# A step list written anew in its first quarter, two fp32 stands a batch instead of three, and scores copied out of PSUM

## The chip, the cores and the metric

The kernel runs on one core of one Trainium2 chip. The metric is the device time of one execution in microseconds (us); three runs of the kernel before gave 703.85, 704.16 and 704.18 us, median 704.16.

## The reference, cut to what matters

```python
# attention over memory slots; B=8 batches, 8 heads, S=576 rows, head dim 64, 32 slots
a = softmax(phi, axis=2)                         # over the rows
k_m, v_m = a^T @ k, a^T @ v                      # 32 slots a head
attn = softmax(q @ k_m^T / 8, axis=-1)           # 576 x 32 a head
x = attn @ v_m                                   # joined to (4608, 512)
h = x @ w_in                                     # (4608, 2048)
g = 0.5 * h * (1 + erf(h / sqrt(2)))
out = g @ w_out                                  # (4608, 512), all in float32
```

## The kernel before, in words

The attention and the first matmul of the feed-forward part are folded together: instead of x the kernel forms U = v_m @ w_in for each batch (32 slots a head, 2048 columns), and h is the product of U and the attention weights p. Both large matmuls keep float32 accuracy by splitting each operand into a high part in FP32R (a float32 format that TensorE takes in one pass) and a low part with the rest, and adding three products: high by high, low by high, high by low.

For a batch b the steps are: load phi, exponentials over the rows (amax, aexp), `slots` (the slot sums k_m and v_m), `km` (scaled copy to SBUF), `slotsT` and `kT` (transposed slots), then for each half of the 576 rows `score` (fp32 matmuls into PSUM), `sT` (transpose by DVE), max, sub, exp, sum, inv, mul, `pT`, and `ph`/`pl` (high and low part of p). `Up.b.f.n` forms n chunks (of 128 columns) of U from chunk f on in fp32, `Uh` and `Ul` split them. For each of 16 chunks f of a batch `h.b.f.hf` is a hidden piece (six FP32R matmuls of 288 columns for one half of the rows), `gelu` writes it to SBUF, `gh`/`gl` split it, and `p.b.f` is a projection (twelve FP32R matmuls of 512 columns into four PSUM banks, acc). `o` copies the sums out. `tp` is the projection of the last 64 rows of two batches. The weights arrive as 64-bit patterns and are decoded once, in the first part, which I call the head: `Lwi.f`/`Lwo.f` load 128 rows, `dB` (two ACT instructions), `dC` (two on DVE), `dS` (DVE), `dDi`/`dDo` (GpSimd, POOL), and for w_out `dE` and `dF`.

The order of all work is written out by hand in ORDER (lines 22 to 202), a list of such steps; the part behind the colon names an engine (a ACT, d DVE) or a kind of PSUM bank (x, y). Lines 1053 to 1057 tie every instruction to the one before it on its engine, the SP queue's DMA issues included, so each engine follows the list strictly, and an instruction that waits holds everything behind it on its engine.

PSUM has eight banks: four for acc (`ps_acc`), two single ones (`ps_h`, kind y), and two that form one tile of a pair (`ps_at`, kind x, line 317). `banks` (line 311) hands them out. A "stand" in this text is a run of fp32 pieces on PE between the FP32R matmuls. From batch 3 on a batch has three: `slots` of the next batch, `score` of half 0 and `Up.b.0.4` (before projection 3 of the batch ahead); `slotsT`, `score` of half 1 and `Up.b.4.4` (before projection 7); `Up.b.8.4` and `Up.b.12.4` (before projection 13). The scores of a half stand in columns 0 to 287 of the two banks, the slot sums of the next batch in columns 384 to 511; `sT` (line 775) and `km` (line 605) read them in PSUM.

SBUF tiles are shared by tag. Tag U (five buffers, NU) holds U tiles, raw weights and later one kv tile a batch; tag kv (eight buffers, NK = NC + 3) holds the ten loads Lkv.1.g.c of batch 1, which slots.1.0 (c of g=0) and slots.1.1 (c of g=1) read (line 569). Warm-up matmuls `W.n` (line 1014) stand in the head where PE would be idle.

Of the kernel before, what the change touches and what calls it, by code (L numbers as in the profile page):

```python
# [23 lines left out]
amax.0.0 aexp.0.0 dC.1.1 Lq.0.0 at.0.0.4 atc.0.0.4:d at.0.0.0 dS.1.1 at.0.1.0 dB.0.1
dC.0.1 dS.0.1 dDo.0 anorm.0 atc.0.1.0:d atc.0.0.0:a Lwi.1 Lwi.0 atc.0.1.4:a dE.0:d
dB.1.0 Lq.0.1 dB.0.0 Lphi.1.0 slots.0.0.0 dF.0 km.0.0.0 slots.0.1.0 Lkv0.1.1 km.0.1.0
Lkv0.0.1 slotsT.0.0 kT.0.0:d dC.1.0 dC.0.0 n_score.0 dS.0.0 dDi.0 n_score.1 n_score.2
n_max.0 n_sub.0 n_exp.0 slots.0.1.1 Lwo.2 Lwi.2 Lkv.1.0.1 amax.1.0 W.1 aexp.1.0 W.3
# [12 lines left out]
max.1.0 Lwi.6 Up.0.4.1 h.0.3.0 dE.4:a Lwo.6 gelu.0.2.1 dC.5.0 gelu.0.2.0 dB.5.1 gh.0.2:a
sub.1.0 exp.1.0 dB.6.1 dF.4 Lwi.7 gl.0.2 dS.5.0 dDi.5 Uh.0.4:d sum.1.0 p.0.1 gelu.0.3.0
Ul.0.4 gelu.0.3.1 Lwo.7 dB.6.0 dC.6.1 Up.0.5.1 dC.5.1 inv.1.0 p.0.2 dS.5.1 Lq.1.1
h.0.4.1 mul.1.0 Uh.0.5:d pT.1.0 dDo.5 Ul.0.5 h.0.4.0 gelu.0.4.1 score.1.1 h.0.5.0
h.0.5.1 dE.5:a dC.6.0 dS.6.0 sT.1.1.1 sT.1.1.0 gh.0.3:a gelu.0.4.0 dDi.6 Up.0.6.1 Lwo.8
gl.0.3 p.0.3 ph.1.0:a dS.6.1 Uh.0.6:a dF.5 Ul.0.6 max.1.1 gh.0.4:a dDo.6 gl.0.4
gelu.0.5.1 Up.1.0.4 Lwo.9 dB.7.0 dE.6:a dC.7.0 h.0.6.1 pl.1.0 gelu.0.5.0 dS.7.0 gh.0.5:a
p.0.4 dDi.7 Uh.1.0 sub.1.1 exp.1.1 Up.0.7.1 Ul.1.0 dB.7.1 gelu.0.6.1 Uh.0.7:a dF.6
h.0.6.0 gl.0.5 p.0.5 sum.1.1 inv.1.1 dC.7.1 dS.7.1 mul.1.1 dB.9.1 Ul.0.7 gelu.0.6.0
dDo.7 h.0.7.0 gelu.0.7.0 pT.1.1 gh.0.6:d h.0.7.1 Up.1.4.4 dC.9.1 gl.0.6 gelu.0.7.1  # L50
ph.1.1:a h.1.0.0 dB.9.0 Lwi.8 dE.7:d gh.0.7:a pl.1.1 gelu.1.0.0 dS.9.1 dB.8.1 p.0.6 dF.7
dB.8.0 h.1.0.1 Uh.1.4:d gl.0.7 gelu.1.0.1 h.1.1.0 dC.9.0 dDo.9 Lwo.10 gh.1.0:a h.1.2.0
dS.9.0 h.1.1.1 dC.8.0 gelu.1.1.0 p.0.7 dC.8.1 dE.9:a dS.8.0 gelu.1.1.1 h.1.2.1 dDi.9
o.0.0.7:a h.1.3.1 gl.1.0 dS.8.1 dF.9 p.1.0 Lwo.11 o.0.1.7:a Ul.1.4 h.1.3.0 gelu.1.2.0
Lwi.10 dDo.8 o.0.2.7:a dB.10.1 h.1.4.1 Lwi.11 gh.1.1:a gelu.1.2.1 o.0.3.7:d dE.8:a
gl.1.1 dDi.8 gelu.1.3.1 dB.10.0 dC.10.1 dS.10.1 dDo.10 gelu.1.3.0 h.1.4.0 gh.1.2:a dF.8
Lwi.14 dB.11.0 gl.1.2 dC.10.0 Lwo.13 p.1.1 Lwi.13 dE.10:d gelu.1.4.0 h.1.5.0 p.1.2
gelu.1.4.1 h.1.5.1 h.1.7.1 dB.11.1 dC.11.0 dF.10 dC.11.1 gh.1.3:a dS.11.1 Lwo.14 gl.1.3
dS.10.0 gelu.1.5.0 dDo.11 dDi.10 p.1.3 h.1.7.0 dB.13.1 dS.11.0 gelu.1.5.1 gh.1.4:d
dDi.11 Up.0.8.4 gl.1.4 gelu.1.7.1 dC.13.1 dE.11:d p.1.4 dF.11 Uh.0.8:a Lwo.12 Lwo.15  # L60
gelu.1.7.0 dB.13.0 h.1.6.1 h.1.6.0 gh.1.5:d dS.13.1 dB.14.1 dDo.13 gl.1.5 Ul.0.8 dC.14.1
h.0.8.0 dS.14.1 h.0.8.1 p.1.5 gelu.1.6.1 dC.13.0 gelu.1.6.0 gh.1.6:a gl.1.6 Up.1.8.4
dB.14.0 gelu.0.8.0 gelu.0.8.1 dS.13.0 h.0.10.1 dDo.14 p.1.6 dC.14.0 dDi.13 Lwi.12
dE.13:d gh.1.7:a h.0.9.0 dE.14:a dF.13 gl.1.7 dS.14.0 Uh.1.8:d dF.14 dB.12.0 dDi.14
p.1.7 dB.12.1 gelu.0.9.0 dC.12.0 dC.12.1 dB.15.1 Lwi.15 gh.0.8:d gl.0.8 dB.15.0 dS.12.0
gelu.0.10.1 Ul.1.8 h.0.10.0 gelu.0.10.0 h.0.9.1 dS.12.1 o.1.2.7:d dDi.12 o.1.1.7:d
dDo.12 gelu.0.9.1 dC.15.0 gh.0.9:a h.0.11.1 Up.0.12.2 o.1.0.7:a h.0.11.0 dS.15.0
o.1.3.7:d gl.0.9 dE.12:d Uh.0.12:d p.0.8 gelu.0.11.0 p.0.9 dC.15.1 gelu.0.11.1 gh.0.10:d
Ul.0.12 dS.15.1 gl.0.10 dDi.15 Lphi.2.1 h.0.13.1 gh.0.11:a dB.15 gl.0.11 Lphin.2
Up.0.14.2 dC.15 h.0.13.0 gelu.0.13.0 Lphi.2.0 Uh.0.14:d amax.2.1 p.0.10 amax.2.0 dF.12  # L70
# [6 lines left out]
gl.1.8 o.0.1.15 Lphi.3.1 Up.1.12.4 gelu.1.10.0 h.1.11.1 Uh.1.12:a p.1.8 gelu.1.10.1
Ul.1.12 slots.2 h.1.11.0 gelu.1.11.1 gelu.1.11.0 km.2.0 km.2.1 gh.1.10:d slotsT.2
amax.3.1 Lphin.3 kT.2:d p.1.9 gl.1.10 score.2.0 Lq.2.1 sT.2.0.1 amax.3.0 h.1.12.1
sT.2.0.0 h.1.12.0 gelu.1.12.0 gelu.1.12.1 Up.2.0.4 p.1.10 max.2.0 Lkv.3.0.3 h.1.13.1  # L80
sub.2.0 aexp.3.1 gh.1.11:d gl.1.11 h.1.13.0 exp.2.0 sum.2.0 inv.2.0 gelu.1.13.0
gelu.1.13.1 Uh.2.0:d gh.1.12:a p.1.11 Ul.2.0 mul.2.0 score.2.1 Lkv.3.0.1 h.1.15.0
# [1041 lines left out]
```

## Time and profile before

| | |
|---|---|
| median of three runs | 704.16 us |
| profiled execution | 704.29 us, span 702.5 us |
| PE busy with matmuls | 687.9 us, 98% of the span |
| DVE, ACT, POOL busy | 400.8, 306.3, 57.0 us |
| granted TensorE clock, mean | 0.997 of full speed |
| moved by DMA | 63.58 MB |

The profile is of one execution. Matmuls are pipelined and their recorded ends are modelled, so a busy PE is one whose matmuls follow each other. L12 is line 12 of the kernel. In a row of the timeline the bracket gives the idle time of the engine ahead of it and what ended it.

### The profile page before, as it was taken

The numbers are of one execution on the slowest core, as the hardware profiler recorded it, in microseconds if no ns is written. First come the engines' busy times: TensorE is split into PE (matmuls) and PEld (weight loads), VectorE is DVE, ScalarE is ACT, GpSimd is POOL, SyncE is SP. The second block draws the span as 40 slices with busy tenths as digits, with TensorE's granted clock in tenths as the row PEclk, the third lists the DMA queues.
The fourth block names the chain that finished last, engine by engine and source line by source line (L and its number), as shares of the span: only waits on it lengthen the run. The fifth ranks groups of instructions, "written<-read, shape, count | busy, mean of one in ns | idle before, by whom it ended". The sixth has DMA issues, their size and how long they took to land.

```text
span 702.5 us, 12355 instructions
## 1 busy us (share of the span) xinstructions
PE 687.9 (98%) x4970; PEld 574.4 (82%) x4970; DVE 400.8 (57%) x757; ACT 306.3 (44%) x692; POOL 57.0 (8%) x42
## 2 busy tenths in 40 slices
...
GB/s 341 341 279 113 121 151 192 61 47 201 132 139 79 188 155 82 61 51 131 57 1 75 67 118 54 1 61 35 35 0 61 16 35 1 1 61 0 1 1 75
DMA packets 27865, 63.58 MB, mean 91 GB/s; under 512 B 2592, under 2 KB 6432, under 8 KB 27808
## 3 DMA queue, kind: packets, MB, share of 16 engines
...
## 4 chain that ended last, share of the span: by engine, by line
PE 95%; DVE 2%; DMA 1%; ACT 1%; issue 0%; POOL 0%; SPq 0%; ACTq 0%
PE acc L944 50%; PE h L913 29%; PE tacc L944 6%; PE pu L664 4%; PE psc L584 1%; PE psc L664 1%; DMA raw<-w_out 1%; PE psc L683 1%; PE pk L584 1%; PE pk L569 0%; DVE raw L360 0%; DVE s L708 0%; DVE y L366 0%; DVE wo_lo L382 0%; ACT y L354 0%
## 5 line engine op out<-in xcount | busy, mean ns | idle before, releaser
L913 PE MATMUL h<-p_hi,U 128*128 128x288 f32 x1024 | 219.6, 297 | 0.0
L913 PEld LDWEIGHTS h<-p_hi,U 128*128 128x128 f32 x1024 | 169.2, 188 | 10.5 <-issue 3.0
L944 PE MATMUL acc<-wo_hi,gh 128*128 128x512 f32 x512 | 161.4, 395 | 0.0
L944 PE MATMUL acc<-wo_lo,gh 128*128 128x512 f32 x512 | 158.7, 390 | 0.0
L944 PE MATMUL acc<-wo_hi,gl 128*128 128x512 f32 x512 | 158.7, 390 | 0.0
L302 DVE CAST gh<-gf 128x512 fp32r<-128x512 f32 x109 | 47.7, 438 | 187.5 <-PE acc L944 167.0
L913 PE MATMUL h<-p_lo,U 128*128 128x288 f32 x512 | 149.9, 295 | 0.0
L921 ACT ACTIVATE gf<-h 128x288 f32<-128x288 f32 x128 | 52.7, 412 | 184.9 <-PE h L913 157.2
L944 PEld LDWEIGHTS acc<-wo_hi,gh 128*128 128x128 f32 x512 | 92.6, 188 | 31.4 <-issue 14.3
L944 PEld LDWEIGHTS acc<-wo_hi,gl 128*128 128x128 f32 x512 | 96.1, 188 | 20.4
L944 PEld LDWEIGHTS acc<-wo_lo,gh 128*128 128x128 f32 x512 | 96.1, 188 | 19.2
L930 DVE TENSOR_TENSOR gl<-gf,gh 128x512 fp32r<-128x512 f32 x128 | 92.3, 722 | 32.1 <-PE acc L944 23.9
L913 PEld LDWEIGHTS h<-p_lo,U 128*128 128x128 f32 x512 | 96.1, 188 | 2.6
L302 ACT CAST U<-pu 128x512 fp32r<-128x512 f32 (+2 forms) x45 | 27.6, 662 | 73.6 <-PE pu L664 73.5
L923 ACT ACTIVATE gf<-h 128x224 f32<-128x224 f32 x128 | 45.6, 356 | 27.1 <-PE h L913 26.4
L874 DVE TENSOR_TENSOR U<-pu,U 128x512 fp32r<-128x512 f32 (+2 forms) x54 | 40.5, 781 | 10.3 <-ACT U L302 10.1
L664 PE MATMUL pu<-w_in_sb,kT 64*32 64x512 f32 (+2 forms) x624 | 35.1, 519 | 1.7 <-DVE U L874 1.5
L924 ACT ACTIVATE tails<-h 128x64 f32<-128x64 f32 x128 | 28.9, 226 | 7.1 <-DVE gl_t L939 7.1
L376 POOL TENSOR_TENSOR y<-y,raw 128x512 int32<-128x512 int32 x16 | 24.7, 1546 | 58.2 <-DVE y L366 31.4
L360 DVE SCALAR_TENSOR_TENSOR raw<-raw 128x512 int32<-128x512 int32 (+1 forms) x33 | 26.5, 803 | 0.6 <-ACT raw L355 0.3
L354 ACT ACTIVATE y<-raw 128x512 f32<-128x512 f32 (+1 forms) x33 | 22.8, 692 | 8.0 <-DMA raw<-w_in 3.5
L376 POOL TENSOR_TENSOR w_in_sb<-y,raw 128x512 int32<-128x512 int32 x16 | 22.9, 1432 | 34.9 <-DVE y L366 27.5
...
## 6 DMA issues: line engine op xcount, KB each, us to landing
...
```

Of the source, the lines that this page charges most:

```text
L302: return e.copy(dst, src) if e is nc.scalar else e.tensor_copy(dst, src)
L354: nc.scalar.activation(y, high.bitcast(F32), AF.Abs, scale=2.0**16)
L360: nc.vector.scalar_tensor_tensor(low, high, -(2**31), low, op0=ALU.bitwise_and, op1=ALU.bitwise_or)
L376: nc.gpsimd.tensor_tensor(w, y, low, op=ALU.add)
L664: nc.tensor.matmul(ps[g][M * j : M * j + M], st["kT", b][rows, t, M * j : M * j + M], moving[rows, j, :], start=True, stop=True,)
L874: nc.vector.tensor_sub(lo, pu, hi.bitcast(F32))
L913: nc.tensor.matmul(h[:, :HS], u[g][w], x[:, g, :], start=(n == 0), stop=(n == 3 * G - 1))
L921: nc.scalar.activation(gf[:, :HS], h[:, :HS], AF.Gelu)
L923: nc.scalar.activation(gf[:, HS:], h[:, : MAIN - HS], AF.Gelu)
L924: nc.scalar.activation(tails()[:, f, b % 2], h[:, MAIN - HS : HS], AF.Gelu)
L930: nc.vector.tensor_tensor(g_of("gl", b, f), g_of("gf", b, f), g_of("gh", b, f).bitcast(F32), op=ALU.subtract)
L944: nc.tensor.matmul(acc, x, w[:, f, :], start=(first and n == 0), stop=(last and n == 2))
```

## The change

It has three parts. The first quarter of ORDER (up to Ul.1.8) is written anew: the same steps in another order, on other engines here and there, and batch 0's U pieces of chunks 4/5 and 6/7 are joined (Up.0.4.2 and Up.0.6.2 in place of four pieces of one chunk). From batch 3 on a batch has two stands: `slots`, `score` of half 0, `Up.b.0.4` and `Up.b.4.4`; then `slotsT`, `score` of half 1, `Up.b.8.4` and `Up.b.12.4` (before projection 9 or, for batch 3, 11 of the batch ahead). So that the second U piece can use the scores' banks, a new step `sc` copies scores and slot columns (416 columns, 288 in the last batch) to SBUF, bank 0 by DVE and bank 1 by ACT, into tag pT; sT, km and kT then read SBUF. The pair tile ends with the first scores of batch 3, and two single banks (`ps_x`) take its place. The slot columns move to 288 to 415. The tile dg shares the tag of km.

```diff
@@ -20,185 +20,184 @@
 ORDER = """
-Lphi.0.1 amax.0.1 aexp.0.1 Lwo.1 Lphi.0.0 Lwo.0 at.0.1.4 Lkv0.0.0 dB.1.1 Lkv0.1.0
...
-km.0.1.1 Lkv.1.0.0 dB.2.1 n_mul.0 Lkv.1.0.4 n_sum.1 Lkv.1.0.3 km.0.0.1 dDi.1 n_inv.1
-dE.1:a slotsT.0.1 Lwo.3 kT.0.1:a dC.2.1 dB.2.0 n_T.0 dS.2.1 Up.0.0.1 Up.0.1.1 Uh.0.0:a
-n_mul.1 n_sub.2 amax.1.1 Ul.0.0 aexp.1.1 dDo.2 dC.2.0 anorm.1 Lkv.1.0.2 dE.2:a dS.2.0
-dF.1 Lkv.1.1.0 Uh.0.1:a n_T.1 n_exp.2 Lwi.3 W.4 Ul.0.1 n_hi.0 n_sum.2 at.1.0.0 dB.3.1
-n_lo.0 atc.1.0.0:a dC.3.1 Lkv.1.1.3 at.1.1.0 h.0.0.0 Lwo.4 atc.1.1.0:a n_hi.1 dS.3.1
-at.1.1.4 at.1.0.4 n_inv.2 atc.1.1.4:a dDi.2 dB.3.0 gelu.0.0.0 atc.1.0.4:d slots.1.0
-n_mul.2 Lwi.4 km.1.0 n_T.2 Lkv.1.1.2 Lkv.1.1.1 dC.3.0 dS.3.0 Up.0.2.1 Lkv.1.1.4 h.0.1.0
...
-gl.0.0 score.1.0 Lwo.5 p.0.0 dB.5.0 dC.4.0 h.0.3.1 gl.0.1 dS.4.0 sT.1.0.1 sT.1.0.0 dDi.4
...
-h.3.5.1:y gelu.3.5.0 gelu.3.5.1 p.3.2 slots.5:x score.4.0:x gh.3.4:d gl.3.4 Lq.4.1
-sT.4.0.0 sT.4.0.1 Up.4.0.4:y km.5.0 km.5.1 Lkv.6.0.0 Lkv.6.1.0 Lkv.6.0.1 Lkv.6.1.1
-Lkv.6.0.2 Lkv.6.1.2 Lkv.6.0.3 Lkv.6.1.3 max.4.0 Uh.4.0:a sub.4.0 exp.4.0 wg Ul.4.0 p.3.3
...
-gelu.3.9.0 gelu.3.9.1 p.3.6 slotsT.5:x score.4.1:x gh.3.8:d gl.3.8 Lq.5.0 sT.4.1.0
-sT.4.1.1 Up.4.4.4:y kT.5:d Lphin.6 max.4.1 anorm.7 Uh.4.4:a sub.4.1 exp.4.1 wg Ul.4.4
...
-gelu.3.14.1 h.3.15.1:y Lkv5.6 gelu.3.15.0 gelu.3.15.1 p.3.12 Up.4.8.4:x gh.3.14:d
-gl.3.14 Up.4.12.4:y Uh.4.8:a Uh.4.12:a Ul.4.8 Ul.4.12 p.3.13 h.4.0.0:x gh.3.15:d gl.3.15
...
+Lphi.0.1 Lphi.0.0 Lwi.0 amax.0.1 amax.0.0 aexp.0.1 at.0.1.0 aexp.0.0 at.0.0.4 dB.0.0
...
+Lwi.1 slots.0.0.0 Lq.0.0 dB.1.0 W.1 Lq.0.1 km.0.0.0 dS.0.0 dC.1.1 slotsT.0.0 W.4 kT.0.0:d
+Lphi.1.0 n_score.0 dF.0 dC.1.0 dS.1.1 dS.1.0 n_score.1 n_max.0 dDo.1 amax.1.0 n_sub.0
+Lkv0.1.1 Lkv0.0.1 dE.1:a n_max.1 Lwo.2 n_exp.0 W.3 W.8 n_sub.1 Lkv.1.0.3 n_sum.0 n_exp.1
+dF.1 dB.2.1 dDi.1 n_score.2 slots.0.0.1 Lwi.2 dDi.0 n_inv.0 n_sum.1 n_mul.0 n_max.2
+slots.0.1.1 n_inv.1 km.0.1.1 km.0.0.1 slotsT.0.1 kT.0.1:a Lphi.1.1 dC.2.1 n_T.0 dS.2.1
+n_mul.1 dDo.2 aexp.1.0 n_sub.2 dB.2.0 Lwo.4 amax.1.1 Up.0.0.1 n_T.1 Uh.0.0:a Lkv.1.0.4
+n_hi.0 Lwi.3 aexp.1.1 Ul.0.0 Lkv.1.1.1 dE.2:a dC.2.0 dS.2.0 Up.0.1.1 n_lo.0 at.1.1.0
+Uh.0.1:a dDi.2 Lwi.4 at.1.0.0 n_exp.2 n_sum.2 Ul.0.1 dF.2 n_inv.2 Lkv.1.1.4 Lkv.1.0.0
+n_hi.1 Lkv.1.0.2 dB.3.0 dC.3.0 dB.4.1 dB.4.0 n_mul.2 Lkv.1.0.1 dS.3.0 atc.1.1.0:a
+Lkv.1.1.3 h.0.0.0 n_T.2 dC.4.1 at.1.1.4 dC.4.0 Lkv.1.1.0 at.1.0.4 Lwo.5 dS.4.1 anorm.1
+dDo.4 atc.1.0.0:a n_hi.2 Lwo.3 h.0.1.0 atc.1.1.4:a atc.1.0.4:d n_lo.1 gelu.0.0.0 n_lo.2
+dE.4:a slots.1.0 h.0.0.1 Lwi.5 Up.0.2.1 gelu.0.1.0 gelu.0.0.1 Uh.0.2:a km.1.0 dS.4.0
+Lkv.1.1.2 h.0.1.1 dDi.3 dF.4 dB.3.1 gelu.0.1.1 Ul.0.2 gh.0.1:a dB.5.0 dC.3.1 slots.1.1
+km.1.1 h.0.2.1 Up.0.3.1 h.0.2.0 gh.0.0:a dS.3.1 gl.0.1 Uh.0.3:d Ul.0.3 gl.0.0 dDi.4
+gelu.0.2.1 Lq.1.0 slotsT.1 h.0.3.1 dDo.3 kT.1:a gelu.0.2.0 gelu.0.3.1 dB.5.1 dC.5.0
+dS.5.0 Lwo.6 score.1.0 Lwo.7 p.0.0 sT.1.0.1 dDi.5 Up.0.4.2 sT.1.0.0 dE.3:a max.1.0 dC.5.1
...
+Up.0.6.2 gl.0.4 sub.1.1 exp.1.1 pl.1.0 dC.7.1 dS.7.1 dDo.6 gh.0.5:a Uh.0.6:a Ul.0.6 Lwo.8
...
+slots.5:x score.4.0:x gh.3.4:d gl.3.4 Lq.4.1 sc.4.0.0:d sc.4.0.1:a Up.4.0.4:y Up.4.4.4:x
+sT.4.0.0 sT.4.0.1 Lkv.6.0.0 Lkv.6.1.0 Lkv.6.0.1 Lkv.6.1.1 Lkv.6.0.2 Lkv.6.1.2 Lkv.6.0.3
+Lkv.6.1.3 max.4.0 Uh.4.0:a Ul.4.0 Uh.4.4:a Ul.4.4 km.5.0:d km.5.1:d sub.4.0 exp.4.0 wg
...
+gelu.3.11.0 gelu.3.11.1 p.3.8 slotsT.5:y score.4.1:y gh.3.10:d gl.3.10 Lq.5.0 sc.4.1.0:d
+sc.4.1.1:a Up.4.8.4:x Up.4.12.4:y sT.4.1.0 sT.4.1.1 max.4.1 Uh.4.8:a Ul.4.8 Uh.4.12:a
...
@@ -263,7 +262,9 @@
     ops = ctx.enter_context(tc.tile_pool(name="ops", bufs=2))
     ps_acc = ctx.enter_context(tc.tile_pool(name="ps_acc", bufs=1, space=bass.MemoryType.PSUM))
     ps_h = ctx.enter_context(tc.tile_pool(name="ps_h", bufs=2, space=bass.MemoryType.PSUM))
-    ps_at = ctx.enter_context(tc.tile_pool(name="ps_at", bufs=1, space=bass.MemoryType.PSUM))
+    pairs = ctx.enter_context(ExitStack())
+    ps_at = pairs.enter_context(tc.tile_pool(name="ps_at", bufs=1, space=bass.MemoryType.PSUM))
+    single = []
 
 
 
@@ -314,6 +315,16 @@
             name = "_".join(map(str, k))
             if st["engine"] == "y":
                 return [ps_h.tile([P, FB], F32, tag="h", name=f"{name}_{g}") for g in range(G)]
+            if not single and k[0] == "psc" and k[1] > 2:
+                pairs.close()
+                single.append(
+                    pairs.enter_context(
+                        tc.tile_pool(name="ps_x", bufs=2, space=bass.MemoryType.PSUM)
+                    )
+                )
+            if single:
+                x = single[0]
+                return [x.tile([P, FB], F32, tag="x", name=f"{name}_{g}") for g in range(G)]
             t = ps_at.tile([P, G, FB], F32, tag="at", name=name)
             st["pair", *k] = t
             return [t[:, g] for g in range(G)]
@@ -501,7 +512,7 @@
 
     def a_diag(b):
 
-        dg = st["dg", b] = sb.tile([P, G, P], F32, tag="dg", name=f"dg_{b}", bufs=1)
+        dg = st["dg", b] = sb.tile([P, G, P], F32, tag="km", name=f"dg_{b}", bufs=1)
         for g in range(G):
             nc.vector.tensor_scalar_mul(dg[:, g], ident, st["nm", b][:, g : g + 1])
 
@@ -578,7 +589,7 @@
 
         aT, full = st["aT", b], S // P
         ps = banks("psc", b - 1, 0) if b > 3 else banks("pk", b)
-        pk = [x[:, FB - 2 * D :] for x in ps]
+        pk = [x[:, HS : HS + 2 * D] for x in ps]
 
         def product(g, j, w, x, start, stop):
             nc.tensor.matmul(
@@ -611,7 +622,7 @@
     def slots_T(b, *w):
 
         if b > 3:
-            pt = [x[:, FB - P :] for x in banks("psc", b - 1, 1)]
+            pt = [x[:, HS : HS + P] for x in banks("psc", b - 1, 1)]
         else:
             if st["engine"] == "y":
                 pt = ps_h.tile([P, FB], F32, tag="h", name=f"tn_{b}")
@@ -623,10 +634,6 @@
             nc.tensor.transpose(
                 pt[t], st["km", b][:, t].rearrange("p g d -> p (g d)"), ident
             )
-        if b > 3 and ("pair", "psc", b - 1, 1) in st:
-            st["ptk", b] = st["pair", "psc", b - 1, 1][:, :, FB - P :]
-        elif b > 3:
-            st["ptks", b] = pt
 
 
     k_blocks = sb.tile([P, 4, G, M], F32, tag="kT", name="k_blocks", bufs=3)
@@ -643,7 +650,7 @@
                 copy("a", k_blocks[rows, :, g], x)
             return
         if ("ptks", b) in st:
-            for t, x in enumerate(st["ptks", b]):
+            for t, x in st["ptks", b].items():
                 copy("a", kT[:, t], x)
             return
         w = slice(w[0], w[0] + 1) if w else slice(0, 2)
@@ -772,9 +779,22 @@
             ("sT", b, hf),
             lambda: sb.tile([P, G, SB, M], F32, tag="sT", name=f"sT_{b}_{hf}", bufs=1),
         )
-        nc.vector.transpose(
-            sT[:, g].rearrange("p a m -> p (a m)"), st["ps", b, hf, g][:, :HS]
-        )
+        x = st["ps", b, hf, g]
+        nc.vector.transpose(sT[:, g].rearrange("p a m -> p (a m)"), x[:, :HS])
+
+    def s_copy(b, hf, g):
+
+        n = HS if (b + 1 == B) else HS + P
+        raw = tile_of(
+            ("raw_s", b, hf),
+            lambda: sb.tile([P, G, n], F32, tag="pT", name=f"raw_s_{b}_{hf}", bufs=1),
+        )[:, g]
+        copy("da"[g], raw, st["ps", b, hf, g][:, :n])
+        st["ps", b, hf, g] = raw
+        if n > HS and hf == 0:
+            st["pk", b + 1, g] = raw[:, HS:]
+        elif n > HS:
+            st.setdefault(("ptks", b + 1), {})[g] = raw[:, HS:]
 
     def stat(tag, b, hf):
         return tile_of(
@@ -1022,7 +1042,7 @@
         "at": a_T, "atc": a_Tc, "slots": lambda b, *k: slots(b, *k) if k else slots_both(b), "km": slots_m,
         "slotsT": slots_T, "kT": k_T,
         "n_score": score_n, "n_max": n_max, "n_sub": n_sub, "n_exp": n_exp, "n_sum": n_sum,
-        "n_inv": n_inv, "n_mul": n_mul, "n_T": n_T, "n_hi": n_hi, "n_lo": n_lo, "score": score, "sT": s_T, "max": s_max, "sub": s_sub,
+        "n_inv": n_inv, "n_mul": n_mul, "n_T": n_T, "n_hi": n_hi, "n_lo": n_lo, "score": score, "sc": s_copy, "sT": s_T, "max": s_max, "sub": s_sub,
         "exp": s_exp, "sum": s_sum, "inv": s_inv, "mul": s_mul, "pT": p_T,
         "ph": p_hi, "pl": p_lo, "Up": u_p, "Uh": u_h, "Ul": u_l,
         "dB": dec_b, "dC": dec_c, "dS": dec_s, "dDi": lambda f: dec_d(0, f),
```

## Rows read from the trace of the kernel before

**Rows 1.** The page, busy us and share of the span by engine.
```profile
PE 687.9 (98%) x4970; PEld 574.4 (82%) x4970; DVE 400.8 (57%) x757; ACT 306.3 (44%) x692; POOL 57.0 (8%) x42
```

**Rows 2.** Windows, 46 to 702 us: busy by engine, clock, DMA share, GB/s.
```profile
46.00:702.00 656.00, 651.92 (x4492) 545.07 (x4491) 364.86 (x659) 276.33 (x629) 43.64 (x28) 1.00 0.22 74
```

**Rows 3.** Timeline of PE in the head: start, us, engine, line, operation.
```profile
15.33 6.28 PE L683 MATMUL psc<-k_blocks,q 128*128 128x128 f32 x40 [0.89 <-DVE k_blocks L302]
...
35.09 1.43 PE L569 MATMUL pk<-kv,aT 128*32 128x128 f32 x40 [0.67 <-DVE aT L302]
...
39.20 1.43 PE L569 MATMUL pk<-kv,aT 128*32 128x128 f32 x40 [0.66 <-DVE U L874]
...
45.71 0.50 PE L944 MATMUL acc<-wo_hi,gh 128*128 128x512 f32 x1
```

**Rows 4.** Chain of waits around batch 4's third stand: start, us, what.
```profile
355.02 2.72 PE acc L944 x12
357.74 1.88 PE pu L664 x32
359.62 2.94 PE acc L944 x12
```

**Rows 5.** Groups by line, copies of 512 columns out of PSUM.
```profile
L302 DVE COPY o<-acc 128x512 f32<-128x512 f32 x12 | 8.3, 692 | 4.0 <-PE acc L944 4.0
...
L302 ACT COPY o<-acc 128x512 f32<-128x512 f32 x12 | 7.1, 589 | 24.6 <-PE acc L944 24.5
```

**Rows 6.** Timeline of DVE at batch 4's first stand.
```profile
311.65 0.85 DVE L775 STREAM_TRANSPOSE sT<-psc 128x288 f32<-128x288 f32 x2 [2.13 <-PE psc L664]
...
314.36 1.28 DVE L874 TENSOR_TENSOR U<-pu,U 128x512 fp32r<-128x512 f32 x2
...
316.55 0.68 DVE L930 TENSOR_TENSOR gl<-gf,gh 128x512 fp32r<-128x512 f32 x1
```

**Rows 7.** Timeline of PE at the same stand.
```profile
312.33 1.20 PE L944 MATMUL acc<-wo_hi,gh 128*128 128x512 f32 x4
...
321.11 1.07 PE L944 MATMUL acc<-wo_hi,gh 128*128 128x512 f32 x4
```

**Rows 8.** Chain of waits, U pieces of one and of two chunks.
```profile
48.77 0.79 PE h L913 x6
49.56 0.38 PE pu L664 x16
49.94 0.99 PE h L913 x6
...
124.43 0.59 PE pu L664 x16
```

**Rows 9.** Timeline of ACT in the head.
```profile
26.48 0.27 ACT L302 COPY kT<-tn 128x128 f32<-128x128 f32 x1 [0.91 <-PE tn L623]
...
28.40 0.78 ACT L458 ACTIVATE phi<-phi,nm 128x576 f32<-128x576 f32 x1 [0.24 <-DVE nm L452]
...
30.91 0.69 ACT L354 ACTIVATE y<-raw 128x512 f32<-128x512 f32 x1
...
32.07 0.56 ACT L302 COPY aT<-pt 128x512 f32<-128x512 f32 x1
33.37 0.59 ACT L302 COPY aT<-pt 128x512 f32<-128x512 f32 x1 [0.75 <-PE pt L484]
```

**Rows 10.** Windows before and in n_score, columns as in rows 2.
```profile
13.00:14.00 1.00, 0.00 (x0) 0.00 (x0) 1.00 (x3) 0.42 (x1) 0.00 (x0) 1.00 1.04 421
16.00:20.00 4.00, 4.00 (x24) 4.00 (x23) 3.20 (x7) 0.48 (x2) 2.51 (x2) 0.57 1.02 408
```

**Rows 11.** Waits of the SP queue up to 60 us: total, times, longest.
```profile
SPq L403 <- PE pk L569: 7.0, 1, 7.0
```

**Rows 12.** Timeline of the SP queue at 35 to 36 us.
```profile
35.58 0.33 SPq L403 DMA_DIRECT2D kv<-kv  x1
```

**Rows 13.** Window of one us with the DMA engines full, columns as in rows 2.
```profile
41.00:42.00 1.00, 1.00 (x10) 1.00 (x9) 1.00 (x3) 0.94 (x4) 0.23 (x1) 1.00 1.03 397
```

298 lines of the change are left out of this document (145 added, 153 removed).

## The prediction

> **What bounds the kernel now.** I read the page's busy times first, then one window over everything behind the head, PE's timeline in the head, the chain around one batch, and last the queues of ACT and SP. PE (TensorE) is busy 687.9 of 702.5 us [rows 1]; behind 46 us it has 651.92 of 656.00 us in matmuls, and the wait view names nobody it waits for there [rows 2]. So two things can move the time: matmul time (with the changes between fp32 and FP32R pieces) from 46 us on, and the moment at which the first projection p.0.0 starts, 45.71 us [rows 3]. Everything later runs back to back, so a microsecond at p.0.0 is one at the end. DVE and ACT carry 364.86 and 276.33 us in that stretch [rows 2]: not the bound.
>
> The sum is made against the profiled execution, 704.29 us (span 702.5 and 1.79 around it); the median of the runs is 704.16. What a measurement can tell from no change is about 0.2%, 1.4 us.
>
> **Part 1, two stands.** A stand is a run of fp32 pieces between FP32R matmuls; batches 3 to 7 lose their third one. In batch 4 it holds two U pieces, 1.88 us, and the projection behind it takes 2.94 instead of 2.72 us [rows 4]. The U pieces stay (they move into the first two stands, which pay their own border anyway). Only the border goes: 0.22 us a batch, five batches, **-1.1 us**; bounds -0.8 and -1.6.
>
> What the merged stands add is a wait: the second U piece of a stand needs the banks of the scores, free only when DVE and ACT have copied them out. Ten pairs of copies, 416 columns (288 in batch 7), are not in the trace. The nearest rows copy 512 columns out of PSUM, 692 ns on DVE and 589 on ACT [rows 5]; scaled to 416 that is 0.56 and 0.48 us as estimates. In the stand of batch 4 DVE reads the scores from 311.65 us, and behind the first U piece the next matmul begins at 312.33 [rows 6, 7]. A copy from 311.65 ends at 312.21: 0.12 us to spare. I take 0; without scaling (0.69) it would be 0.01 us late, and from both sides I allow 0 to 0.1 for each of ten, up to +1.0. Behind the copy on DVE stand the transposes, the maximum, four subtractions for U (two more, 1.28 us [rows 6]), km, and only then sub, so that sum must wait for exp on ACT (some 0.4). What this could delay is gl of the chunk: it ends now at 317.2, and its projection starts at 321.11 [rows 6, 7], 3.9 us to spare. Of these 0.56 + 1.28 + 0.4 = 2.2 go, and 0.9 come back as the stand is longer by one U piece; 2.6 stay, so I cost it at nothing. If that cover went, every microsecond would be one of PE. The DMAs in these batches move with their stands, and the next batch's buffers come free as before.
>
> **Part 2, joined U pieces.** On the chain a piece of 128 columns takes 0.38 us (at 49.56), one of 256 takes 0.59 (at 124.43), and a hidden piece behind a U piece 0.99 instead of 0.79 [rows 8]. Joining saves 2 x 0.38 - 0.59 = 0.17 and one border, 0.2, together 0.37; twice, **-0.7 us**. All of it lies on PE behind p.0.0.
>
> **Part 3, the head's new order,** worked out in four steps.
> a) Up to the first copy of kT, which ACT starts at 26.48 now [rows 9]. n_score starts at about 15.1 instead of 15.33 (W.1 and W.4 now stand ahead of it; q has landed). It took 6.28 us for 40 records [rows 3], because the mean granted clock from 16 to 20 us was 0.57, near the lower level of 1.2 GHz (0.50), after PE had done nothing from 13 to 14 [rows 10]. That cost 4 x (1 - 0.57) = 1.7 us. With the gaps filled it may stay at 2.4 GHz; between 0 and 1.7 us gained I take the middle, 0.8, as the new list fills some of that gap and not all. With W.1 (0.2) moved ahead: kT at 25.3, -1.2.
> b) From there ACT is dense. It started kT at 26.48 and slots.1.0 began at 35.09 [rows 3, 9], 8.6 us. The new list puts two more decode pairs ahead of the copies (each as 30.91 to 32.07, 1.16) and aexp.1.0 (0.78), while the two waits of 0.24 and 0.75 us are filled [rows 9]; on PE it puts h.0.1.0 ahead of slots.1.0, about 1.0. That is 2.3 + 0.8 - 1.0 + 1.0 = +3.1, so slots.1.0 begins at 35.1 - 1.2 + 3.1 = 37.0.
> c) **The DMA queue** is the step that decides. Tag kv has eight buffers and batch 1 needs ten. The ninth load waited 7.0 us on PE's slots.1.0 (L569) and went out at 35.58, 0.5 us behind its start [rows 11, 12]. Now the ninth and the tenth followed each other, and slots.1.1 ran at 39.20 [rows 3]. In the new list SP has Lkv.1.1.0 (ninth), Lwo.5, Lwo.3, Lwi.5, Lkv.1.1.2 (tenth). All five are held until 37.5, and the tenth's bytes stand behind three weight pieces: 0.26 + 3 x 0.52 + 0.26 = 2.1 MB at about 400 GB/s (397 at 41 to 42 us [rows 13]) are 5.2 us. With about 1 us until bytes move (estimate) and 0.5 to the signal, the tenth lands at 44.2. PE can fill from 37.0 only slots.1.0, two hidden pieces and a U piece, 3.9 us: it stands still from 40.9, **+3.3 us**.
> d) From slots.1.1 to p.0.0 now are 6.5 us (39.20 to 45.71 [rows 3]) with four hidden pieces; in the new list three, 5.7, and two chunks of slots.1.1 (0.5) can run ahead of the wait. So p.0.0 starts at 44.2 + 5.7 - 0.5 = 49.4, +3.7. By then seven hidden pieces are done instead of six: -0.8. Head: +2.9.
>
> Behind p.0.0 the head's weight decoding keeps its amount; DVE and ACT were not waited for and get 3.7 us of lead. dg moves to tag km: its reader on POOL is done long before km is written. No cost.
>
> **Sum:** -1.1 - 0.7 + 2.9 = +1.1, and 704.29 + 1.1 = 705.4. The bounds of a) move it by 0.8 either way. Those of b) are 0.7 either way: the two waits (0.24 and 0.75) may be filled only in part, and h.0.1.0 may lie beside ACT's decoding for as much.
>
> **Rivals.**
> *The loads come in time.* If the tenth load lands by 41 (slots.1.0 two us earlier, or bytes of kv not kept behind the weights), the 3.3 us of step c go: 705.4 - 3.3 = 702.1, faster. For it: wide margins in b), and today's wait of 7.0 us on SP shows no kv load in front of slots.1.1, which waited for DVE (0.66) [rows 3]. Against: all loads leave by one queue, SP's, in list order, and the ninth demonstrably waited. Chance 0.34.
> *The clock falls.* The profile shows a mean of 0.57 from 16 to 20 us, behind a PE that had stood still from 13 to 14 [rows 10]. The new pause of 3.3 us in front of slots.1.1 is longer than that. A fall of the same size costs 1.7 us, all on PE's path; together with no gain in a), 0.8, the time is 705.4 + 1.7 + 0.8 = 707.9, slower. It decides as soon as the pause in front of slots.1.1 is followed by a granted clock under 1.00, as the gap at 13 was. The Trainium skill ("TensorE: Matmul & The Clock Gate", section "Part 1: The HAM clock gate (the "warmup" mystery)") says that the throttled clock is the default state and that activity releases it; by that rule a pause like this one would be paid for with 707.9 instead of 705.4, and the trace agrees with its 0.57. Against: the rows show one such fall, which is too little to tell how often a pause like it brings one. Chance 0.22.
> *The copies are late in each stand.* With 0.3 us more than estimated (DVE still at gl, or bank and copy handed over late) PE would wait 0.2 in ten places: 705.4 + 2.0 = 707.4, slower, and the merged stands would be worth less than nothing. Against: in the stand of batch 4 DVE had been idle for 2.13 us before the scores [rows 6]. Chance 0.08.
>
> **How the numbers follow.** The forecast, 705.4, has 0.36; its own range is 703.4 to 708.2 if all bounds above fall one way; most of it lies within 1.4 us of no change, so I count it as the same. Faster: the first rival, 0.34. Slower: 0.22 + 0.08 = 0.30. The range that should hold 8 in 10 reaches from 701.4 (first rival with the 0.7 of step b) to 708.2 (second rival with some of the copies' bound).
>
> **What would show it.** Right: behind the head the third stand is gone, no wait of PE on DVE or ACT in front of the second U piece; in the head an SP wait on L569, a PE wait on a kv DMA in front of slots.1.1 at about 41 to 44 us, p.0.0 near 49.4. Wrong: p.0.0 at 47 or earlier (first rival), granted clock under 1.00 between 43 and 50 us (second), PE waits for L302 inside stands (third). If p.0.0 comes before 45.7, step b or c is wrong altogether.

## The result, and the profile after

The changed kernel takes 709.63 us (median of five runs, 708.96 to 711.53) against 704.16 (the median of the five runs beside it too): a ratio of 1.0077, 95% interval 1.0063 to 1.0092. It is slower by 5.5 us. 705.4 was forecast, with a range up to 708.2; the measured time lies above it.

The profiled execution after is the slowest of its five, 711.53 us, span 709.8; before it was 704.29 and 702.5. The two profiles are 7.24 us apart, and the sums below are made against that. First PE's timeline of the changed kernel from slots.1.0 to the first projection (start, us, engine, line, operation; in the bracket the idle time ahead of it and what ended it). It answers to [rows 3].

```profile
38.30 1.43 PE L580 MATMUL pk<-kv,aT 128*32 128x128 f32 x40
...
42.52 0.64 PE L580 MATMUL pk<-kv,aT 128*32 128x128 f32 x16 [0.41 <-DMA kv<-kv]
47.22 1.66 PE L580 MATMUL pk<-kv,aT 128*32 128x128 f32 x24 [4.06 <-DMA kv<-kv]
48.81 0.61 PE L933 MATMUL h<-p_hi,U 128*128 128x288 f32 x1
...
55.50 0.50 PE L964 MATMUL acc<-wo_hi,gh 128*128 128x512 f32 x1
```

The reader is to see two things. PE waits 4.06 us in the middle of slots.1.1, for a kv load. And the 24 matmul records behind that wait take 1.66 us, where 40 took 1.43 us at 38.30. p.0.0 starts at 55.50 instead of 45.71, 9.79 us later. The last matmul row of the timeline tells what lies behind it, first of the kernel before, then of the changed one:

```profile
697.54 0.39 PE L944 MATMUL tacc<-wo_hi,gl_t 128*128 128x512 f32 x1
```

```profile
704.78 0.39 PE L964 MATMUL tacc<-wo_hi,gl_t 128*128 128x512 f32 x1
```

From p.0.0 to the start of this matmul it was 697.54 - 45.71 = 651.83 us, and now it is 704.78 - 55.50 = 649.28: 2.55 less. So 9.79 lost in the head minus 2.55 gained behind it is the whole difference of 7.24.

The waits of PE in the changed kernel (us in total, times, longest) show the same: the four largest rows all belong to the head, and only the first is behind 33 us.

```profile
PE pk L580 <- DMA kv<-kv: 4.5, 2, 4.1
PE pk L568 <- DMA w_in_sb<-kv: 4.1, 1, 4.1
PE pt L495 <- DVE U L894: 2.4, 1, 2.4
PE pt L495 <- ACT phi L469: 1.0, 1, 1.0
```

The SP queue of the changed kernel, from 38 to 44 us, answers to [rows 12] (L414 issues kv loads, L350 pieces of w_out, L346 pieces of w_in):

```profile
38.79 0.33 SPq L414 DMA_DIRECT2D kv<-kv  x1
39.21 2.02 SPq L350 DMA_DIRECT2D raw<-w_out  x2
41.29 0.42 SPq L346 DMA_DIRECT2D raw<-w_in  x1
41.81 0.38 SPq L414 DMA_DIRECT2D kv<-kv  x1
```

The ninth kv load goes out 0.5 us behind the start of slots.1.0 (38.30), then Lwo.5, Lwo.3 and Lwi.5, and the tenth load at 41.81, in the order of the list. Windows of one us (busy time of PE, PEld, DVE, ACT and POOL, then granted clock, DMA share, GB/s), as in [rows 10]:

```profile
38.00:39.00 1.00, 1.00 (x30) 0.83 (x32) 0.61 (x4) 0.99 (x2) 1.00 (x2) 1.00 0.00 0
39.00:40.00 1.00, 1.00 (x26) 0.60 (x16) 0.20 (x1) 0.98 (x3) 0.80 (x1) 1.00 0.55 43
...
43.00:44.00 1.00, 0.16 (x8) 0.00 (x0) 0.00 (x0) 0.00 (x0) 0.00 (x0) 1.00 1.03 381
44.00:45.00 1.00, 0.00 (x0) 0.00 (x0) 0.00 (x0) 0.00 (x0) 0.00 (x0) 0.90 0.97 365
45.00:46.00 1.00, 0.00 (x0) 0.00 (x0) 0.15 (x1) 0.84 (x2) 0.00 (x0) 0.50 1.07 380
...
48.00:49.00 1.00, 1.00 (x17) 0.39 (x10) 0.05 (x1) 0.91 (x2) 0.00 (x0) 0.50 0.97 391
...
54.00:55.00 1.00, 1.00 (x12) 0.71 (x19) 0.09 (x1) 0.24 (x2) 0.78 (x1) 0.50 0.00 0
55.00:56.00 1.00, 1.00 (x18) 0.46 (x3) 0.30 (x1) 1.00 (x4) 0.52 (x1) 0.98 0.00 0
```

From 43 to 45 us no compute engine but PE's last matmuls has anything to do: PE waits for the kv load, ACT for a piece of w_out (3.57 us, until 45.16) and DVE for ACT. The clock falls to 0.50 (1.2 GHz) at about 45, while PE stands still, and stays there while PE works from 47 to 55.

The part behind the head is as forecast in its sum. PE, DVE and ACT at the first stand of batch 4 in the changed kernel, which answers to [rows 6, 7]:

```profile
319.65 2.03 PE L671 MATMUL pu<-w_in_sb,kT 64*32 64x512 f32 x32
```

```profile
319.95 0.59 DVE L303 COPY raw_s<-psc 128x416 f32<-128x416 f32 x1 [2.11 <-PE psc L671]
```

```profile
319.99 0.51 ACT L303 COPY raw_s<-psc 128x416 f32<-128x416 f32 x1 [5.09 <-PE psc L671]
```

The two U pieces of the stand follow each other in one run of 32 records, 2.03 us, with the copies (0.59 and 0.51 us) beside the first of them. The wait view has the copies only at PE's weight loads (PEld):

```profile
PEld pu L671 <- ACT raw_s L303: 7.2, 10, 0.8
```

That is ten times 0.7 us, one for each stand, and for most of it PE itself has the first U piece's matmuls to do. But not for all of it. The weight loads of the second piece start when DVE's copy has ended (319.95 + 0.59 = 320.54), and in batch 7, whose copies have 288 columns instead of 416, the pair of U pieces is shorter:

```profile
320.55 0.22 PEld L671 LDWEIGHTS pu<-w_in_sb,kT 64*32 64x32 f32 x16 [0.74 <-ACT raw_s L303]
```

```profile
569.32 1.92 PE L671 MATMUL pu<-w_in_sb,kT 64*32 64x512 f32 x32
```

The pair takes 2.03 us (once 2.10) in the eight stands that copy 416 columns, and 1.92 in the two of batch 7. So the copies hold PE up by about 0.1 us in each of eight stands, too little to show in PE's own waits.

### The profile page after: what moved, and what is told of

Its sections match the earlier page's. It is cut to its first block, busy times and chain, and to the rows that moved or that the text cites. A ratio compares the mean times of both kernels' runs of the same rounds, so it can differ in the third digit from the quotient of the medians.

```text
span 709.8 us, 12323 instructions
## 1 busy us (share of the span) xinstructions
PE 689.9 (97%) x4938; PEld 577.9 (81%) x4938; DVE 405.2 (57%) x773; ACT 312.2 (44%) x706; POOL 56.8 (8%) x42
## 4 chain that ended last, share of the span: by engine, by line
PE 96%; DMA 2%; ACT 1%; SPq 0%; issue 0%; DVE 0%; ACTq 0%
PE acc L964 50%; PE h L933 29%; PE tacc L964 6%; PE pu L671 4%; PE psc L595 1%; PE psc L671 1%; DMA w_in_sb<-kv 1%; DMA kv<-kv 1%; PE pw L1034 1%; PE psc L690 1%; PE pk L568 1%; PE pk L595 1%; PE pk L580 0%; ACT y L365 0%; ACT raw L366 0%; ACT phi L469 0%
## 5 line engine op out<-in xcount | busy, mean ns | idle before, releaser
L933 PE MATMUL h<-p_hi,U 128*128 128x288 f32 x1024 | 222.1, 300 | 0.0
L933 PEld LDWEIGHTS h<-p_hi,U 128*128 128x128 f32 x1024 | 171.7, 191 | 8.5 <-issue 3.0
L933 PEld LDWEIGHTS h<-p_lo,U 128*128 128x128 f32 x512 | 97.6, 191 | 2.6
L528 POOL PARTITION_ALL_REDUCE pn<-dg x5 | 9.1, 1812 | 203.1 <-DVE dg L517 136.9
L964 PE MATMUL tacc<-wo_hi,gl_t 128*128 128x512 f32 x64 | 25.0, 390 | 0.0
```

The source lines that it names most:

```text
L933: nc.tensor.matmul(h[:, :HS], u[g][w], x[:, g, :], start=(n == 0), stop=(n == 3 * G - 1))
L964: nc.tensor.matmul(acc, x, w[:, f, :], start=(first and n == 0), stop=(last and n == 2))
```

## The experiments

Line numbers differ by a few between the kernels, as the list takes more or fewer lines. In all rows below, "from p.0.0" is the time from the first projection to the start of the last matmul in that run's timeline. Each ratio is taken against runs of the kernel before that were made beside the experiment; their medians were 704.63 us (experiments 1 and 2 and the first kernel of 3), 704.85 (the second of 3, and 4, 6 and 7) and 705.13 (5 and 8). These differ by half a microsecond and more, and so may medians of different experiments.

**1. Split the change in two.** One kernel has the old first quarter (without the joins) and the new stands, the other the new first quarter and the old stands.

```
e1: ORDER = [first quarter of before, up to Ul.1.8] + [rest of after]; code of after
e2: ORDER = [first quarter of after,  up to Ul.1.8] + [rest of before]; code of before
```

> Old first quarter of the list (with the four U pieces not joined), new stands from batch 3 on. Theory 'the head pays, the stands gain': p.0.0 starts near 45.7 us as in the kernel before and the stands give 1.1 us back, bounds 0 to 1.6: 702.6 to 704.2 us, most likely 703.1. Rival 'the copies are late in each stand': ten waits of PE of 0.2 us or more on the copies (L303) in front of a second U piece, 705.2 us or more.

> New first quarter of the list (with the joined U pieces), the three old stands. Theory 'the head pays': p.0.0 at 53 to 56 us as in the changed kernel, and the time 709.6 plus the 1.1 us that the stands no longer give: 710 to 711.5 us. Rival 'the copies are late in each stand': the head is paid for only in part, and without the copies the time is 707.5 us or less.

The old first quarter with the new stands took 703.42 us, ratio 0.9982 (0.9970 to 0.9994); the new first quarter with the old stands 710.92, ratio 1.0084 (1.0062 to 1.0106). From p.0.0 the first needs 697.99 - 47.52 = 650.47 and the second 705.34 - 54.97 = 650.37, against 651.83 before and 649.28 with both parts. So the stands give 1.4 us alone and 1.1 beside the new head, and the new head with its joins takes 1.5 or 1.2 off what lies behind p.0.0. All the loss is in the new first quarter; no rival of the stands is needed. (The p.0.0 of the first kernel lies at 47.52 and not at 45.7 in its profile: n_score began 0.46 us later there and took 7.61 us instead of 6.28, with the clock at 0.50 from 10 to 22 us. Its median of twelve runs is 1.3 us below its profiled execution.)

**2. The place of one load.** The tenth kv load moves to right behind the ninth.

```diff
-dS.4.0 Lkv.1.1.2 h.0.1.1
+dS.4.0 h.0.1.1
-Lkv.1.1.0 at.1.0.4 Lwo.5
+Lkv.1.1.0 Lkv.1.1.2 at.1.0.4 Lwo.5
```

> The changed kernel with one load moved: the tenth kv load stands right behind the ninth, ahead of the three weight pieces. Theory 'the queue': both loads land by about 43 us, the pause of PE in front of the last part of slots.1.1 (4.1 us) is gone, and with it the fall of the clock behind it (some 4 us): p.0.0 near 47.5 us, 701 to 703 us. If only the pause goes and the clock still falls: 705 to 706. Rival 'bytes, not order': the weight pieces are late in turn and the decoding behind them (L365) holds gelu and gh, so that p.0.0 still starts behind 52 us and the time stays over 707.

709.93 us, ratio 1.0063 (1.0044 to 1.0083): nothing is gained. The pause in front of the last part of slots.1.1 is gone, and another has come behind it. PE's timeline of this kernel:

```profile
41.41 1.77 PE L582 MATMUL pk<-kv,aT 128*32 128x128 f32 x40
...
48.89 0.68 PE L673 MATMUL pu<-w_in_sb,kT 64*32 64x128 f32 x16 [4.73 <-DVE km L618]
```

The chain of waits of the same kernel says why:

```profile
39.08 0.82 SPq L416
...
40.43 6.08 DMA raw<-w_out
...
46.53 0.66 ACT y L367
47.19 0.58 ACT raw L368
...
47.79 0.69 DVE raw L373
48.49 0.27 DVE km L618
```

The load is Lwo.3. It stands in SP's queue behind the held kv loads as well, goes out at about 40.4 and lands at 46.51. Its decoding, dB.3.1 on ACT and dC.3.1 on DVE, stands ahead of km.1.1 in the list; km must wait for it, and PE for km. So the rival named in the expectation was right in that the decoding behind a weight piece holds PE; it does so through km, where the rival had gelu and gh. The queue's hold reaches PE by **two paths**, and with one of them cut the other is as long. The waits of PE in the changed kernel show only the later one of the two.

**3. The price of the clock.** Warm-up matmuls on PE ahead of slots.1.1, where PE stands still.

```diff
-dB.5.0 dC.3.1 slots.1.1
+dB.5.0 dC.3.1 W.36 slots.1.1      (second run: W.18)
```

> The changed kernel with 36 warm-up matmuls on PE (about 4.3 us) directly ahead of slots.1.1, where PE stands still; the pause itself stays. Theory 'half the loss behind the pause is the clock': the granted clock stays at 1.00 from 43 to 56 us, the 8 us of work from slots.1.1 to p.0.0 take 4 us less, p.0.0 near 51.5 us, and the time is 705 to 706.5. Rival 'the pause alone': DMA or DVE set p.0.0 there, the clock plays no part, and the time stays within 0.7 us of 709.6.

> The changed kernel with 18 warm-up matmuls ahead of slots.1.1 (36 records by the count of the run with 36, which had 72 records in 8.2 us, so about 4.1 us), no longer than the pause. Theory 'the clock behind the pause costs some 3 us': granted clock 1.00 from 43 us on, slots.1.1 ends at about 48, p.0.0 near 52.5 us, 706 to 707.5 us. Rival 'the pause alone': p.0.0 stays behind 54.5 us and the time within 0.7 us of 709.6.

The first of them was mis-sized: 36 warm-ups are 72 records and took 8.20 us, so slots.1.1 began at 49.82, behind its load, and the 711.38 us tell nothing about the clock. The second, with 18, took 708.35 us, ratio 1.0047 (1.0030 to 1.0064). Its timeline of PE:

```profile
41.67 4.18 PE L1036 MATMUL psc<-one 128*128 128x128 f32 x36
45.78 0.64 PE L582 MATMUL pk<-kv,aT 128*32 128x128 f32 x16
46.84 1.00 PE L582 MATMUL pk<-kv,aT 128*32 128x128 f32 x24 [0.42 <-DMA kv<-kv]
...
52.14 0.50 PE L966 MATMUL acc<-wo_hi,gh 128*128 128x512 f32 x1
```

The granted clock stays at 1.00 from 42 us on. The same work from the last part of slots.1.1 to p.0.0 takes 52.14 - 46.84 = 5.30 us, and in the changed kernel 55.50 - 47.22 = 8.28: the clock behind the pause costs 3.0 us in the profiled execution. That price is not the same in each: in the profile of the new first quarter with the old stands (experiment 1), which has the same pause, the same work took 54.97 - 47.53 = 7.44 us, 2.1 more than at full clock.

```profile
47.53 1.67 PE L568 MATMUL pk<-kv,aT 128*32 128x128 f32 x24 [4.27 <-DMA kv<-kv]
...
54.97 0.50 PE L943 MATMUL acc<-wo_hi,gh 128*128 128x512 f32 x1
```

The time fell by 1.3 us between the medians, 3.3 between the profiles (of the changed kernel the slowest of five executions was profiled), and by the two ratios about 2.1. p.0.0 is where it was expected, the time 0.9 above the expected range. The pause itself is as long as ever and is the larger part: p.0.0 is still 52.14 - 45.71 = 6.4 us later than before the change.

**4. The hold itself taken away.** The list stays as it is; the two kv loads that found no free buffer land in columns of w_in's tile that are decoded much later.

```diff
+        if (b, g, c) in ((1, 1, 0), (1, 1, 2)):
+            n = 2 * ((b, g, c) == (1, 1, 2))
+            t = w_in_sb[:, n : n + 2, DFF - 4 * D :].rearrange("p a (j d) -> p a j d", j=4)
+        else:
+            t = ops.tile([P, 2, 4, D], F32, tag="kv", ...)
```

> The changed kernel, list untouched, but two of batch 1's ten kv loads (group 1, chunks 0 and 2, those that found no free kv buffer) land in columns of w_in's tile that are decoded much later. So SP no longer waits for slots.1.0, and neither the tenth kv load nor the weight pieces Lwo.5 and Lwo.3 behind it are held. Theory 'the hold of SP's queue is the whole loss at 42 us, by two ways (the kv load, and the decoding of Lwo.3 that stands ahead of km)': neither the wait of PE on a kv load (4.1 us) nor that on km (4.7 us) is left, p.0.0 at 46.5 to 48.5 us, and with 656 us from there to the end 702.5 to 704.5 us. Rival 'ACT and DVE have too much decoding in the head': a wait of 3 us or more stays in front of p.0.0, which starts behind 51 us, and the time stays over 707.

702.98 us, ratio 0.9975 (0.9964 to 0.9986). The whole loss is gone, and the kernel is 1.8 us faster than the one before. Its timeline of SP, and then of PE:

```profile
31.25 0.60 SPq L418 DMA_DIRECT2D w_in_sb<-kv  x1
32.15 1.71 SPq L350 DMA_DIRECT2D raw<-w_out  x2
34.10 0.33 SPq L346 DMA_DIRECT2D raw<-w_in  x1
34.47 0.56 SPq L418 DMA_DIRECT2D w_in_sb<-kv  x1
```

```profile
37.29 1.43 PE L584 MATMUL pk<-kv,aT 128*32 128x128 f32 x40
...
46.95 0.50 PE L968 MATMUL acc<-wo_hi,gh 128*128 128x512 f32 x1
```

These loads go out 7.1 to 7.5 us earlier, and p.0.0 starts at 46.95. So neither DVE nor ACT has too much to do in the new head; the held queue is the cause of the loss.

**5. The list alone mended.** The two weight pieces go ahead of the held load; kv's buffers stay eight.

```diff
-Lkv.1.1.0 at.1.0.4 Lwo.5 dS.4.1 anorm.1 dDo.4 atc.1.0.0:a n_hi.2 Lwo.3 h.0.1.0
+Lwo.5 Lwo.3 Lkv.1.1.0 Lkv.1.1.2 at.1.0.4 dS.4.1 anorm.1 dDo.4 atc.1.0.0:a n_hi.2 h.0.1.0
```

(with Lkv.1.1.2 taken from its old place)

> The changed kernel with the list alone mended, kv buffers as they were: Lwo.5 and Lwo.3 go out ahead of the ninth kv load, which SP still holds until slots.1.0, and the tenth follows the ninth directly. Theory 'two paths through one held queue, the tenth load and Lwo.3's decoding': both kv loads land by about 42 us, Lwo.3 long before; PE waits less than 1.5 us in front of slots.1.1 and not at all on km; p.0.0 at 47 to 48.5 us, 703 to 704.5 us. Rival 'the two loads need places of their own': PE still waits 3 us or more between slots.1.0 and p.0.0, 706 or more.

703.93 us, ratio 0.9982 (0.9970 to 0.9993). The kv loads are still held until slots.1.0, but nothing stands behind them that PE needs soon. PE's timeline:

```profile
37.73 1.43 PE L582 MATMUL pk<-kv,aT 128*32 128x128 f32 x40
...
41.53 1.57 PE L582 MATMUL pk<-kv,aT 128*32 128x128 f32 x40
...
48.39 0.50 PE L966 MATMUL acc<-wo_hi,gh 128*128 128x512 f32 x1
```

This settles the cause, together with experiment 4: the loss needs both a load that waits for a buffer and loads behind it that PE needs soon. A place of its own for each of the two loads ends it, and so does moving the others ahead.

**6. The same places in the old list.**

```diff
+        if (b, g, c) in ((1, 1, 1), (1, 1, 4)):
```

(the rest as in experiment 4, with the list of the old first quarter and the new stands)

> The old first quarter with the new stands, and the two kv loads that found no free buffer there (group 1, chunks 1 and 4) landing in w_in's columns too. Theory 'in the old list the hold costs nothing, since slots.1.1 waited on DVE': within 0.7 us of the old first quarter with the new stands (703.4). Rival 'the hold cost the old list as well, by the weight pieces behind it': p.0.0 a microsecond or more earlier, 702.4 or less.

704.37 us, ratio 0.9991 (0.9979 to 1.0004), against 703.42 with kv's own buffers; the intervals overlap, the difference of 0.95 is 0.25 above what I allowed, and nothing is gained. The 7.0 us of hold in the kernel before [rows 11] cost nothing that these runs show, as slots.1.1 waited there on DVE. From p.0.0 this kernel needs 650.89 us, 0.4 more than its twin in experiment 1, so the gain of the stands alone is known only as 0.9 to 1.4 us.

**7. The earlier fall of the clock.** In the new list PE stands still from 30.0 to 32.4 us, and the clock is 0.50 behind that. Nine warm-ups were put there, with the two kv loads in w_in's columns.

```diff
-dC.2.0 dS.2.0 Up.0.1.1 n_lo.0 at.1.1.0
+dC.2.0 dS.2.0 Up.0.1.1 n_lo.0 W.9 at.1.1.0
```

> As the run with the two kv loads in w_in's columns (new list), and 9 warm-up matmuls (18 records, 2.1 us) in the pause of PE at 30.0 to 32.4 us, behind which the clock fell to 0.50 until 38 us. Theory 'this fall costs PE 2 to 3 us before slots.1.0': clock 1.00 from 30 us on, p.0.0 1.5 to 3 us earlier than without them, 700 to 702.5 us. Rival 'ACT sets slots.1.0 (it is dense from 26 to 36 us)': the clock stays up, but slots.1.0 starts less than 0.7 us earlier, and the time is within 0.7 us of the run without them.

703.17 us, against 702.98 without them. The clock stayed at 1.00 from 26 us on (without the warm-ups it was 0.50 from 32 to 35 us), and slots.1.0 began at 37.09 instead of 37.29: the rival was right. ACT, which PE waits for in front of it (1.54 us at 35.95), sets that moment. Half a clock there costs next to nothing.

**8. The copies of the scores.** The second U piece of each stand goes to the bank kind that the scores don't use.

```diff
-sc.4.0.0:d sc.4.0.1:a Up.4.0.4:y Up.4.4.4:x
+sc.4.0.0:d sc.4.0.1:a Up.4.0.4:y Up.4.4.4:y
-sc.4.1.0:d sc.4.1.1:a Up.4.8.4:x Up.4.12.4:y
+sc.4.1.0:d sc.4.1.1:a Up.4.8.4:x Up.4.12.4:x
```

(likewise in batches 3, 5, 6 and 7)

> The run with the two kv loads in w_in's columns, and in batches 3 to 7 the second U piece of each stand in the free bank of the kind that the scores don't use (y in the first stand, x in the second), so that it no longer waits for the copy of the scores. In the changed kernel such a pair of U pieces took 2.03 us, in the kernel before 1.95. Theory 'the copy is 0.08 us late in each of ten': the pair takes 1.95 us, and from p.0.0 to the last matmul PE needs 0.8 us less than the 649.2 us of the other runs with both parts. Rival 'nothing is late, or the next hidden piece now waits for its bank': 649.1 us or more.

740.67 us, ratio 1.0527 (1.0492 to 1.0562). I had taken a U piece to fill one bank; it fills both of its kind, one for each half of the heads, so the second piece now waits for the reading of the first. PE's timeline in batch 4's first stand:

```profile
317.37 1.06 PE L675 MATMUL pu<-w_in_sb,kT 64*32 64x512 f32 x16
320.57 1.68 PE L675 MATMUL pu<-w_in_sb,kT 64*32 64x512 f32 x16 [2.13 <-DVE U L898]
```

Both theories missed this. Ten such waits are 21.2 us (PE's wait view has 21.9 in eleven; the eleventh, 0.8 us, belongs to the head and stands in the other runs too). From p.0.0 this kernel needs 38.0 us more than the run of experiment 4. Of these, 21.2 are the waits; the second piece takes at least 1.68 us behind a wait instead of 1.06, ten times about 0.6; and in six places the granted clock falls to 0.50 with PE busy for some 3 to 4 us, which comes to about 10 us lost. The run shows from the other side what the copies of the change are worth: they free the second pair of banks. It could not test the 0.08 us by which such a pair takes longer (2.03 us against 1.95 for the two U pieces of the third stand before); the 1.92 us of batch 7 in the changed kernel, with its shorter copies, say that the copies are late by that much.

## Why the prediction was wrong, step by step

**What bounds the kernel** was right: nothing but p.0.0's moment and the matmul time behind it moved the time.

**Parts 1 and 2** were right in mechanism and in their sum. Forecast behind p.0.0: -1.1 for the stands, -0.7 for the joins, -0.8 for one hidden piece done earlier, together -2.6; measured -2.55. The stands are 0.9 to 1.4 by the split. The joins were not tried alone: with the hidden piece they are 1.2 to 1.6, where 1.5 was counted. The copies were estimated at 0.56 and 0.48 us and took 0.59 and 0.51; they were costed at nothing and hold PE up by about 0.1 us in each of eight stands, within the bound of 0 to 0.1. So the borders that went must be worth more than the 0.22 us counted for each, and that the sum agrees so closely is partly luck.

**Part 3** is what failed: step d) counted no fall of the clock behind the pause, step c) took the landing of the first held load too short, and step a) looked past a load. Part 3 put p.0.0 at 49.4; the profile has 55.50, 6.1 later. (Between the median and the forecast there are 4.2 us; the profiled execution is 1.9 above its median.) The 6.1 us fall on three terms:

- Step a) said kT 1.2 us earlier, at 25.3. ACT started it at 26.66, 0.2 later than before. What the step did not look at is a load of w_in_sb: PE waited 4.1 us for it, slots.0 began at 11.10 instead of 9.96, and n_score at 16.43 instead of the 15.1 forecast. From there to kT it was 26.66 - 16.43 = 10.2 us, as forecast (25.3 - 15.1). **+1.3**, and slots.1.0 is at 38.30 instead of 37.0 for that reason alone: step b's way from kT to it, 11.7 us, came out as 38.30 - 26.66 = 11.6. (In the kernels of experiments 1, 2, 3 and 5 with the new first quarter slots.1.0 is at 37.6 to 38.05, so up to half of this term belongs to the one execution.) The clock, which I let rise, had a mean of 0.66 from 10 to 20 us (0.83 before), but that does not explain the term: the 80 matmuls of slots.0 took 2.89 us at a granted clock of 0.50, and 2.92 in the kernel before, where the rows show 1.00 from 10 to 13 us (later there, at 21.54, 40 such matmuls took 0.90). So it is not shown either that the 0.57 in step a came from a fall behind the gap at 13 us; PE had been as slow ahead of that gap. First the row of the kernel before, then two of the changed one:

```profile
9.96 2.92 PE L557 MATMUL pk<-w_in_sb,aT 128*32 128x64 f32 x80
```

```profile
11.10 2.89 PE L568 MATMUL pk<-w_in_sb,aT 128*32 128x64 f32 x80 [4.09 <-DMA w_in_sb<-kv]
...
16.43 4.26 PE L690 MATMUL psc<-k_blocks,q 128*128 128x128 f32 x32
```

- Step c), the queue, was the right mechanism: five loads in the forecast's order, held until 0.5 us behind slots.1.0, the tenth last. The bytes between the ninth and the tenth were right too: 1.83 MB at 400 GB/s are 4.6 us, and their landings are 47.18 - 42.5 = 4.7 apart. Wrong was the first landing. I counted 1 us until bytes move, 0.65 for the bytes and 0.5 to the signal, 2.2 in all; the ninth took about 3.7 (38.79 to 42.5), and the window from 39 to 40 moved 43 GB/s only. From slots.1.0 to the tenth's landing it is 8.9 instead of 7.2: **+1.7**. No row stood behind the 1 us and the 0.5, and the kernel before had a row that speaks against them: its ninth load, sent at 35.58 into a stretch that had no traffic either, took 3.4 us from issue to landing. In the other kernels that keep this order (experiments 1 and 3) the ninth lands after 2.8 to 3.1 us, but the tenth lands 8.3 to 8.9 us behind the ninth's issue, as here (8.4), where 6.7 was forecast; so the excess is firm, and its split between the two loads is not. The ninth load in the DMA view of the kernel before (issues from 35 to 36 us; KB each, us to landing):

```profile
kv<-kv SPq DMA_DIRECT2D x1, 256.0 KB, 3.4
```

- Step d) had 5.2 us from that landing to p.0.0, with the clock at full speed. At full clock it is 5.30 (experiment 3); it took 8.28. This is the second rival, and its mechanism came true: **+3.1**, of which 3.0 are the clock. I priced it at 1.7 from a fall of 4 us with a mean of 0.57, and gave it 0.22. The pause in front of slots.1.1 is 4.06 us and not 3.3, and behind it PE worked some 8 us at 0.50.

1.3 + 1.7 + 3.1 = 6.1. The new first quarter with the old stands (experiment 1) shows the same three in other shares: slots.1.0 at 38.04 (+1.0), the tenth load used at 47.53 (+2.3) and p.0.0 at 54.97 (+2.2). So the forecast (step c) and the second rival (the clock) both happened, and each of them was larger than it was priced. The upper end, 708.2, was made of the rival's price and part of the copies' bound, and held nothing for step c: I had bounded a) and b), and left the latency of the first load and the length of the slow stretch without a bound. What the Trainium skill says ("TensorE: Matmul & The Clock Gate", section "Part 1: The HAM clock gate (the "warmup" mystery)"), that the throttled clock is the default state and that activity releases it, agrees with the trace in that the clock fell to 0.50 while PE stood still, and stayed at 1.00 where 18 warm-ups filled the pause. That PE's work from 47 us on had the full clock back only at 55 us is told by the rows alone.

**The first rival** was half right. It had the tenth load land by 41, and p.0.0 then at 49.4 - 3.3 = 46.1. With both queue paths open it lands in time and p.0.0 is at 46.95. But the load alone is not enough: I had not seen that Lwo.3's decoding stands ahead of km.1.1 and hangs on the same queue (experiment 2). In the changed kernel itself this cost nothing, since the kv load was as late. **The third rival**, the copies 0.2 us late in ten places, did not occur: they are late by about 0.1 us in eight, and the stands still brought what was forecast.

The new first quarter is a good list: with the hold taken away it is worth as much as the old one, and with the new stands the kernel runs at 0.9975 of the time before and 0.9975 / 1.0077 = 0.990 of the changed one.
